# A second feed-forward whose split of g is issued one step later, with the last check and the last stores moved

## The chip, the cores and the metric

The kernel runs on one core of one Trainium2 chip. The metric is the device time of one execution in microseconds. TensorE multiplies matrices into PSUM; ScalarE and VectorE do element-wise work and copy results out of PSUM; GpSimd issues gathers; SyncE (SP) issues most of the other transfers. Each engine works through its own list of instructions, in the order of the program, and waits for the others by semaphores.

## The reference

Three parts follow one another: a gated linear attention, a mixture of eight experts with the best two for each token, and a second feed-forward. The change lies in the last.

```python
def _moe2_ref(x, w_in, w_out):       # x: 3072 x 384, w_in: 384 x 2048, w_out: 2048 x 384
    h = x @ w_in
    g = h - np.tanh(h)
    return (g @ w_out).astype(np.float32)

attn_out = _attn_ref(**attn_kwargs)  # 4 x 8 heads, 768 tokens, 48 wide
x = attn_out.transpose(0, 2, 1, 3).reshape(3072, 384)
x = _moe_ref(x=x, **moe_kwargs)      # 8 experts, 1024 wide, best 2 of each token
return _moe2_ref(x=x, **moe2_kwargs)
```

## The kernel before

The function `fast` holds all three parts. Numbers are kept as pairs of 16-bit halves, a high one and a low one that holds the rest, so that a product takes three 16-bit matmuls: high by high, high by low, low by high.

The second feed-forward cuts the 3072 tokens into six blocks of 512 (`blk`) and the 2048 hidden columns into sixteen groups of 128 (`f`). That gives M = 96 steps, numbered n = 16 blk + f. In step n:

- `ff_first` makes the **first products**: nine matmuls of 512 columns on TensorE (line 185) into a PSUM bank `ph`. Four banks take turns. ScalarE then makes `z` from `ph` (line 637, with a sum over the columns into `hsum`), and `s` from `z` (638). VectorE makes `s` (639) and `g` (641). z(n), s(n), g(n) are those of step n.
- `ff_split` splits `g`: ScalarE writes the **high half** of the tile `hs` (line 647), then VectorE the **low half** (648). Four tiles `hs` take turns.
- `ff_second` makes the **second products** of step n - 3 (FF_LAG = 3): twelve matmuls of 384 columns (line 200), three for each of four groups of 128 tokens, into the banks `py0` to `py3`. The third of each three reads the low half. After f = 15 the block is done: the four banks are copied to tiles `o`, two by ScalarE (line 665) and two by VectorE (663), and each is stored by a transfer that SP issues (666). The next block's second products for f = 0 need the same four banks.
- Then come extras of the step: `combine`, `put_m` and `sum_m` prepare the tokens of the next block and sum them, `weight_sum` (line 149) sums weights, and in the last block one piece of `checks` a step tests the value ranges.

Order on an engine is program order, which the loop at the end of `fast` writes out by hand. first(n) and second(n) are the two kinds of product of step n; the second feed-forward starts behind the last step of the experts, and steps 0 to 3 have first products ahead of second(0).

When the last step's sums are there, `last_check` makes one column `ok` in six small VectorE operations; a tiny matmul counts it, and VectorE writes `flag` (line 816). All engines load the flag (line 1064) and branch on it (1065): where a check fails, a general version (`general`) runs behind the branch. In every execution here it is jumped over.

Of the kernel before, what the change touches and what calls it, by code (L numbers as in the profile page):

```python
# [20 lines left out]
B, H, S, D = 4, 8, 768, 48  # L21
N, DM, NE, FF, F2 = 3072, 384, 8, 1024, 2048
# [44 lines left out]
def rows(ap, offset, pattern):  # L67
    return bass.AP(tensor=ap.tensor, offset=ap.offset + offset, ap=pattern)
# [3 lines left out]
def fast(ctx, tc, flag, f_cols, kq_cols, v_rows, gates, blank, w12, w_in, w_out, out):  # L72
    nc = tc.nc
# [12 lines left out]
    ones = consts.tile([128, 128], BF, name="ones")  # L86
# [61 lines left out]
    def weight_sum(e, f, i):  # L148
        nc.scalar.activation(junk[:, :DM], RING[e, f][:, 0, 3 * i:3 * i + 3, :].rearrange("p a b -> p (a b)"),  # L149
                             AF.Square, accum_out=wsum[:, 8 * e + f, i:i + 1])  # L150
# [17 lines left out]
    def new_xt(key):  # L168
        XT[key] = xtp.tile([128, 6, 512], F16, name="xt")
# [9 lines left out]
    def first_products(ph, n, lhs, key):  # L179
        x = XT[key]  # L180
        o = 0
        for a in range(3):
            wh, wl = lhs(a)
            for l, r in ((wh, a), (wh, 3 + a), (wl, a)):
                nc.tensor.matmul(ph[:, :n], l, x[:, r, :n], start=(o == 0), stop=(o == 8))  # L185
                o += 1

    def second_products(key, f, last, rhs, parts):
        hs = HS.pop((key, f))
        wh, wl = (w.rearrange("p a b -> p (a b)") for w in rhs)  # L190
        for i, (c0, m) in enumerate(parts):
            if f == 0:
                PY[key, i] = ps.tile([128, DM], F32, name=f"py{i}", tag=("b0", "b1", "b2", "b5")[i])
            p = PY[key, i]
            if m == 64:
                ops = [(hs[:, c0:c0 + 2 * m], w) for w in (wh, wl)]
            else:
                ops = [(hs[:, s + c0:s + c0 + m], w) for s, w in ((0, wh), (0, wl), (512, wh))]
            for o, (l, r) in enumerate(ops):
                nc.tensor.matmul(p[:max(m, 128)], l, r, start=(f == 0 and o == 0),  # L200
                                 stop=(f == last and o == len(ops) - 1))
# [401 lines left out]
    YG = {}  # L603

    def gather_y(j):
        g1, g2 = (late.tile([128, DM], F32, name=f"g{r}", bufs=6) for r in range(2))
        for r, g in ((0, g1), (1, g2)):
            nc.gpsimd.indirect_dma_start(out=g, out_offset=None, in_=y_rows if j > 3 else y_rows[:Y_EARLY],  # L608
                                         in_offset=bass.IndirectOffsetOnAxis(ap=yslot[:, r, j:j + 1], axis=0))
        YG[j] = (g1, g2)  # L610

    def combine(j):
        g1, g2 = YG.pop(j)
        nc.scalar.activation(g1, g1, AF.Copy, scale=wt[:, 0, j:j + 1])  # L614
        nc.vector.scalar_tensor_tensor(g1, g2, wt[:, 1, j:j + 1], g1, op0=OP.mult, op1=OP.add)
        YG[j] = g1

    def put_m(j):
        g1 = YG.pop(j)
        m = late.tile([128, 2 * DM], F16, name="m16")  # L620
        nc.scalar.activation(m[:, :DM], g1, AF.Copy)
        nc.vector.tensor_tensor(m[:, DM:], g1, m[:, :DM], op=OP.subtract)
        c = 128 * (j % 4)
        nc.sync.dma_start_transpose(XT["m", j // 4][:, :, c:c + 128], m)
        YG[j] = g1

    def sum_m(j):
        nc.scalar.activation(junk[:, :DM], YG.pop(j), AF.Square, accum_out=msum[:, j:j + 1])  # L628

    def ff_first(blk, f):  # L630
        ph = ps.tile([128, 512], F32, name="ph", tag=next(tags["ph"]))
        first_products(ph, 512, lambda a: (winS[:, 0, a, f * 128:(f + 1) * 128],
                                           winS[:, 1, a, f * 128:(f + 1) * 128]), ("m", blk))
        z = ff.tile([128, 512], F32, name="z")
        s = ff.tile([128, 512], F32, name="s")
        i = blk * 16 + f
        nc.scalar.activation(z, ph, AF.Square, scale=SZ ** 0.5 / SH, accum_out=hsum[:, i:i + 1])  # L637
        nc.scalar.activation(s, z, AF.Square, scale=1.0 / SZ, bias=bias_a)  # L638
        nc.vector.scalar_tensor_tensor(s, s, ZD, z, op0=OP.add, op1=OP.mult)  # L639
        g = ff.tile([128, 512], F32, name="g")  # L640
        nc.vector.scalar_tensor_tensor(g, s, 0.5, ph, op0=OP.mult, op1=OP.mult)  # L641
        YG["g", blk, f] = g

    def ff_split(blk, f):
        g = YG.pop(("g", blk, f))
        hs = tiles.tile([128, 1024], F16, name="hs", bufs=4)
        nc.scalar.activation(hs[:, :512], g, AF.Copy)  # L647
        nc.vector.tensor_tensor(hs[:, 512:], g, hs[:, :512], op=OP.subtract)  # L648
        HS[("m", blk), f] = hs

    def ff_second(blk, f):
        w = RING[NE, f // 2]
        c = 3 * (f % 2)
        second_products(("m", blk), f, 15, (w[:, 0, c:c + 3, :], w[:, 1, c:c + 3, :]),
                        [(128 * i, 128) for i in range(4)])
        if f < 15:
            return
        for i in range(4):
            c, b = divmod(4 * blk + i, B)
            o = ff.tile([128, DM], F32, name="o", bufs=4)  # L660
            p = PY.pop((("m", blk), i))
            if i % 2:
                nc.vector.tensor_scalar(o, p, 2.0 * C2 / (SH * SZ * SW), None, op0=OP.mult)
            else:
                nc.scalar.activation(o, p, AF.Copy, scale=2.0 * C2 / (SH * SZ * SW))  # L665
            nc.sync.dma_start(rows(out, (b * S + c * 128) * DM, [[DM, 128], [1, DM]]), o)

    todo = [(1, i) for i in range(32)] + [(0, 8 * a + c) for c in range(8) for a in range(3)]
    loads_ahead = list(todo)
# [1 line left out]
    for n in range(3, len(moe_steps) + LAG):  # L671
# [3 lines left out]
        e, blk, f = moe_steps[n]  # L675
# [52 lines left out]
    def holds(i, src, bound, op):  # L728
        t = held[:, :src.free_size()]
        if len(src.shape) > 2:  # L730
            t = t.rearrange("p (a b) -> p a b", b=src.shape[2])
        nc.vector.tensor_scalar(t, src, bound, None, op0=op)
        nc.vector.tensor_reduce(okay[:, i:i + 1], held[:, :src.free_size()], axis=AX.X, op=OP.min)
# [5 lines left out]
    def check(i, src, bound, op):  # L739
        holds(i, src, bound, op)  # L740
        both(okay[:, i:i + 1])
# [48 lines left out]
    def last_check():  # L790
        check(2, hsum[:, 90:], HMIN2 * SZ, OP.is_ge)
        holds(3, hsum[:, 90:], HMAX2 * SZ, OP.is_le)
        ok = consts.tile([128, 1], BF, name="ok")
        nc.vector.tensor_tensor(ok, okay[:, 0:1], okay[:, 3:4], op=OP.mult)
        return ok
# [3 lines left out]
    FF_LAG = 3  # L799
    steps = [(blk, f) for blk in range(6) for f in range(16)]  # L800
    M = len(steps)
    halves = [(e, f, i) for e in (NE - 1, NE) for f in range(8) for i in range(2)]
    checking = checks()
    for n in range(M + FF_LAG):
        if n < M:
            blk, f = steps[n]
            ahead = 4 * blk + 4
            if blk < 5 and f == 0:
                for i in range(4):
                    gather_y(ahead + i)  # L810
                new_xt(("m", blk + 1))
            ff_first(blk, f)
        if n == M + FF_LAG - 1:
            p = ps.tile([1, 1], F32, name="pt", tag="b7")
            nc.tensor.matmul(p, ok, ones[:, 0:1], start=True, stop=True)
            nc.vector.tensor_scalar(flag, p, 128.0, None, op0=OP.is_lt)
        if n >= FF_LAG:
            ff_second(*steps[n - FF_LAG])
        if n >= M:
            continue  # L820
        ff_split(blk, f)
        if blk < 5:
            if f in (1, 3, 5, 7):
                combine(ahead + f // 2)
            if f in (2, 4, 6, 8):
                put_m(ahead + f // 2 - 1)
            if f in (9, 10, 11, 12):
                sum_m(ahead + f - 9)
        else:
            next(checking, None)  # L830
        if halves and (blk == 5 or f == 0 or f > 12):
            weight_sum(*halves.pop(0))
        if n < 2:
            sum_m(2 * n)
            sum_m(2 * n + 1)
        if n == M - 1:
            ok = last_check()


@with_exitstack  # L840
# [218 lines left out]
def fused_kernel(tc, args, packed, out):  # L1059
    nc = tc.nc  # L1060
    with tc.tile_pool(name="flags", bufs=1) as flags:
        flag = flags.tile([1, 1], I32, name="flag")
        fast(tc, flag, *packed, *args[-2:], out)
        again = nc.values_load(flag, min_val=0, max_val=1)
        with tc.If(again > 0):
            general(tc, *args, out)
# [54 lines left out]
```

## Time and profile before

| | us |
|---|---|
| median of 3 runs | 971.24 |
| lowest and highest run | 967.05, 971.27 |
| the profiled execution, its own time | 962.48 |
| its span in the trace | 960.7 |
| TensorE busy | 938.4 (98%) |
| VectorE busy | 616.0 (64%) |
| ScalarE busy | 611.2 (64%) |
| GpSimd busy | 160.5 (17%) |

The trace is of one execution, whose own time is less than that of all three runs that were timed without a profile. The second feed-forward runs from about 568 us to the end of the span. In the rows PE is TensorE, PEld its weight loads, ACT ScalarE, DVE VectorE, POOL GpSimd and SP SyncE. A name with a q (SPq) is the engine's queue of instructions that are not counted as busy: issues of transfers, semaphores, branches. "Idle before" is how long an engine stood before an instruction, and the arrow names what ended the wait. The granted clock of TensorE is 1.00 at its full speed.

### The profile page before, as it was taken

To read this page: it belongs to the slowest core of one execution; us is meant where nothing else is said; L and a number is where in the kernel's file an instruction comes from. 1 tells how busy PE (TensorE), PEld (TensorE's weight loads), DVE (VectorE), ACT (ScalarE), POOL (GpSimd) and SP (SyncE) were. 2 spreads that over 40 slices of the span, in tenths; PEclk is the share of its full clock that TensorE was granted. 3 is DMA by queue.
4 is the path that set the end of the run, shared out by engine and by line. 5 is a ranking of instruction groups with operands and counts; after the bars stand their busy time and mean duration, and the time that the engine had idled before them with its cause. 6 is when DMAs were issued, how large, how long until landed. Compare 5 with 4: busy or idle time off the path is not lost.

```text
span 960.7 us, 16309 instructions
## 1 busy us (share of the span) xinstructions
PE 938.4 (98%) x5970; PEld 576.5 (60%) x5970; DVE 616.0 (64%) x1274; ACT 611.2 (64%) x1593; POOL 160.5 (17%) x194
## 2 busy tenths in 40 slices
PE   8999998999999999999999999979999999999996
PEld 8999986555656565656556554535555555555553
DVE  8999995466464646566666556556566565665764
ACT  7777763575757575776767566666665666666663
POOL 2387786000000000000000223200301201000000
PEclk9999999999999999999999999989999999999999
DMA  7877855756565456564645354212222121110001
GB/s 274 286 248 252 263 166 170 200 176 167 153 177 149 161 143 187 151 157 134 186 122 136 99 149 103 64 34 44 74 42 47 44 58 42 42 26 1 33 1 37
DMA packets 111801, 120.03 MB, mean 125 GB/s; under 512 B 66400, under 2 KB 89568, under 8 KB 111584
## 3 DMA queue, kind: packets, MB, share of 16 engines
q1 hardware_dynamic: 105568, 100.03, 36.4%
q0 software_dynamic: 6144, 18.88, 6.3%
q8 instruction: 48, 0.79, 0.3%
q14 instruction: 41, 0.34, 0.1%
HBM read 76.41 MB, written 29.88 MB: 111 GB/s over the span
## 4 chain that ended last, share of the span: by engine, by line
PE 60%; ACT 21%; DVE 14%; issue 1%; DMA 1%; POOL 0%; SPq 0%; DVEq 0%; ACTq 0%
PE py L200 24%; PE ph L185 23%; ACT s L638 6%; DVE s L639 6%; DVE g L641 6%; ACT hs L647 5%; ACT z L637 5%; PE pY L366 4%; PE pA L339 2%; PE pt L410 2%; PE pY L364 2%; PE pK L383 2%; ACT junk L628 1%; ACT junk L149 1%; ACT g L614 1%
## 5 line engine op out<-in xcount | busy, mean ns | idle before, releaser
L200 PE MATMUL py<-wsplit,hs 128*128 128x384 f16 x2432 | 433.8, 327 | 7.2 <-ACT o L665 5.6
L200 PEld LDWEIGHTS <-hs 128*128 128x128 f16 x2432 | 237.0, 98 | 181.3 <-issue 9.2
L185 PE MATMUL ph<-xt,wsplit 128*128 128x512 f16 (+3 forms) x1152 | 223.5, 339 | 0.4 <-DMA xt<-xs 0.4
L185 PE MATMUL ph<-xt,winS 128*128 128x512 f16 x864 | 201.7, 379 | 0.0
L185 PEld LDWEIGHTS <-wsplit 128*128 128x128 f16 x1152 | 112.5, 98 | 86.7 <-DMA xt<-xs 0.8
L218 DVE SCALAR_TENSOR_TENSOR hs<-ph,hs 128x256 f16<-128x256 f32 (+2 forms) x192 | 79.6, 443 | 119.1 <-ACT hs L210 118.9
L608 POOL DMA_INDIRECT g<-y_rows,yslot x48 | 52.7, 1097 | 585.1 <-ACT wsplit L144 376.0
L210 ACT ACTIVATE hs<-ph 128x512 f16<-128x512 f32 (+3 forms) x128 | 65.8, 514 | 132.6 <-PE ph L185 132.6
L647 ACT ACTIVATE hs<-g 128x512 f16<-128x512 f32 x96 | 60.4, 629 | 138.5 <-DVE g L641 138.5
L185 PEld LDWEIGHTS <-winS 128*128 128x128 f16 x864 | 84.4, 98 | 92.0
L639 DVE SCALAR_TENSOR_TENSOR s<-s,z 128x512 f32<-128x512 f32 x96 | 66.5, 692 | 80.9 <-ACT s L638 80.9
L648 DVE TENSOR_TENSOR hs<-g,hs 128x512 f16<-128x512 f32 x96 | 66.4, 692 | 63.3 <-ACT hs L647 61.9
L145 DVE SCALAR_TENSOR_TENSOR wsplit<-raw,wsplit 128x768 f16<-128x768 f32 x72 | 70.3, 976 | 16.3 <-ACT wsplit L144 15.0
L149 ACT ACTIVATE junk<-wsplit 128x384 f16<-128x384 f16 x144 | 74.4, 516 | 2.3
L638 ACT ACTIVATE s<-z,bias_a 128x512 f32<-128x512 f32 x96 | 69.3, 722 | 3.1
L641 DVE SCALAR_TENSOR_TENSOR g<-s,ph 128x512 f32<-128x512 f32 x96 | 65.9, 687 | 3.3
L144 ACT ACTIVATE wsplit<-raw 128x768 f16<-128x768 f32 x72 | 59.9, 832 | 0.3 <-DMA raw<-wo_f 0.3
L479 POOL DMA_INDIRECT xs<-xkeep,yslot x48 | 55.7, 1161 | 15.8 <-issue 8.7
L637 ACT ACTIVATE z<-ph 128x512 f32<-128x512 f32 x96 | 55.4, 577 | 2.0 <-PE ph L185 1.9
L366 PE MATMUL pY<-v,am 128*128 128x48 f32 x384 | 53.3, 267 | 0.0
L366 PEld LDWEIGHTS pY<-v,am 128*128 128x128 f32 x384 | 49.6, 192 | 0.1
L325 POOL TENSOR_TENSOR kqT<-eneg,kq 128x512 f32<-128x512 f32 x23 | 32.0, 1392 | 16.0 <-ACT eneg L321 15.7
(135 smaller groups left out, 904.9 us busy)
## 6 DMA issues: line engine op xcount, KB each, us to landing
raw<-in_w SPq DMA_DIRECT2D x64, 384.0 KB, 3.8
kq<-in_kq_cols SPq DMA_DIRECT2D x24, 512.0 KB, 5.8
y_rows<-yo SPq DMA_DIRECT2D x47, 192.0 KB, 1.9
f<-in_f_cols SPq DMA_DIRECT2D x24, 256.0 KB, 4.3
w<-in_moe_w_out SPq DMA_DIRECT2D x32, 192.0 KB, 3.4
w<-in_moe_w_in SPq DMA_DIRECT2D x24, 256.0 KB, 3.4
v<-in_v_rows SPq DMA_DIRECT2D x24, 192.0 KB, 3.2
out<-o SPq DMA_DIRECT2D x24, 192.0 KB, 2.0
```

What stands on the lines that cost most here:

```text
L145: nc.vector.scalar_tensor_tensor(t[:, 1], raw, SW, t[:, 0], op0=OP.mult, op1=OP.subtract)
L149: nc.scalar.activation(junk[:, :DM], RING[e, f][:, 0, 3 * i:3 * i + 3, :].rearrange("p a b -> p (a b)"), AF.Square, accum_out=wsum[:, 8 * ...
L185: nc.tensor.matmul(ph[:, :n], l, x[:, r, :n], start=(o == 0), stop=(o == 8))
L200: nc.tensor.matmul(p[:max(m, 128)], l, r, start=(f == 0 and o == 0), stop=(f == last and o == len(ops) - 1))
L218: nc.vector.scalar_tensor_tensor(hs[:, at:at + hi - lo], ph[:, lo:hi], 0.0, hs[:, lo:hi], op0=OP.max, op1=OP.subtract)
L366: nc.tensor.matmul(pY[:, at + 48 * s:at + 48 * s + 48], am[:, s, a, :], vt[:, 2 * a + s, :], start=not c, stop=bool(s) or not c)
L637: nc.scalar.activation(z, ph, AF.Square, scale=SZ ** 0.5 / SH, accum_out=hsum[:, i:i + 1])
L638: nc.scalar.activation(s, z, AF.Square, scale=1.0 / SZ, bias=bias_a)
L639: nc.vector.scalar_tensor_tensor(s, s, ZD, z, op0=OP.add, op1=OP.mult)
L641: nc.vector.scalar_tensor_tensor(g, s, 0.5, ph, op0=OP.mult, op1=OP.mult)
L647: nc.scalar.activation(hs[:, :512], g, AF.Copy)
L648: nc.vector.tensor_tensor(hs[:, 512:], g, hs[:, :512], op=OP.subtract)
```

## The change

Three edits in the second feed-forward. The split of step n - 1 is issued in step n, behind the first products and the element-wise work of step n and ahead of the second products of step n - 3. `last_check` is issued inside the last `ff_first`, behind the last z and s of ScalarE and ahead of the last s of VectorE; the matmul on its result and the write of the flag come one step earlier, ahead of second(94). And the stores of the last block that belong to ScalarE's copies are issued by ScalarE.

```diff
@@ ff_first
         nc.scalar.activation(s, z, AF.Square, scale=1.0 / SZ, bias=bias_a)
+        if i == 95:
+            YG["ok"] = last_check()
         nc.vector.scalar_tensor_tensor(s, s, ZD, z, op0=OP.add, op1=OP.mult)
@@ ff_second
-            nc.sync.dma_start(rows(out, (b * S + c * 128) * DM, [[DM, 128], [1, DM]]), o)
+            (nc.sync if i % 2 or blk < 5 else nc.scalar).dma_start(
+                rows(out, (b * S + c * 128) * DM, [[DM, 128], [1, DM]]), o)
@@ the loop over n
             ff_first(blk, f)
-        if n == M + FF_LAG - 1:
+        if 0 < n <= M:
+            ff_split(*steps[n - 1])
+        if n == M + FF_LAG - 2:
             p = ps.tile([1, 1], F32, name="pt", tag="b7")
-            nc.tensor.matmul(p, ok, ones[:, 0:1], start=True, stop=True)
+            nc.tensor.matmul(p, YG["ok"], ones[:, 0:1], start=True, stop=True)
             nc.vector.tensor_scalar(flag, p, 128.0, None, op0=OP.is_lt)
         if n >= FF_LAG:
             ff_second(*steps[n - FF_LAG])
         if n >= M:
             continue
-        ff_split(blk, f)
...
-        if n == M - 1:
-            ok = last_check()
```

The lines behind the edits move by two or three: what is 647, 648, 663, 665 and 816 before is 649, 650, 665, 667 and 821 after.

**ScalarE at the end of block 0.** The rows are those of the steps n = 17 and 18; `py0` and `py2` hold the results of block 0, `g0` and `m16` are tiles of the extras. Before:

```order
L637 ACTIVATE z_7417,hsum_92<-ph_7407 128x512
L638 ACTIVATE s_7418<-z_7417,bias_a_74 128x512
L647 ACTIVATE hs_7436<-g_7422 128x512
L614 ACTIVATE g0_7357<-g0_7357,wt_91 128x384
L637 ACTIVATE z_7451,hsum_92<-ph_7441 128x512
L638 ACTIVATE s_7452<-z_7451,bias_a_74 128x512
L665 ACTIVATE o_7470<-py0_6929 128x384
L665 ACTIVATE o_7476<-py2_6937 128x384
L647 ACTIVATE hs_7482<-g_7456 128x512
L621 ACTIVATE m16_7485<-g0_7357 128x384
```

After:

```order
L637 ACTIVATE z_7414,hsum_92<-ph_7404 128x512
L638 ACTIVATE s_7415<-z_7414,bias_a_74 128x512
L649 ACTIVATE hs_7421<-g_7386 128x512
L614 ACTIVATE g0_7354<-g0_7354,wt_91 128x384
L637 ACTIVATE z_7448,hsum_92<-ph_7438 128x512
L638 ACTIVATE s_7449<-z_7448,bias_a_74 128x512
L649 ACTIVATE hs_7455<-g_7419 128x512
L667 ACTIVATE o_7470<-py0_6929 128x384
L667 ACTIVATE o_7476<-py2_6937 128x384
L621 ACTIVATE m16_7482<-g0_7354 128x384
```

In step 17 the high half is now that of the step before (it reads `g_7386`, not the `g_7419` of its own step), and in step 18 it stands ahead of the two copies `o`, where it stood behind them.

**VectorE at the same place.** `s_7452` (before) and `s_7449` (after) are those of n = 18. Before:

```order
L639 SCALAR_TENSOR_TENSOR s_7452<-s_7452,z_7451 128x512
L641 SCALAR_TENSOR_TENSOR g_7456<-s_7452,ph_7441 128x512
L663 TENSOR_SCALAR o_7473<-py1_6933 128x384
L663 TENSOR_SCALAR o_7479<-py3_6941 128x384
L648 TENSOR_TENSOR hs_7482<-g_7456,hs_7482 128x512
L622 TENSOR_TENSOR m16_7485<-g0_7357,m16_7485 128x384
```

After:

```order
L641 SCALAR_TENSOR_TENSOR s_7449<-s_7449,z_7448 128x512
L643 SCALAR_TENSOR_TENSOR g_7453<-s_7449,ph_7438 128x512
L650 TENSOR_TENSOR hs_7455<-g_7419,hs_7455 128x512
L665 TENSOR_SCALAR o_7473<-py1_6933 128x384
L665 TENSOR_SCALAR o_7479<-py3_6941 128x384
L622 TENSOR_TENSOR m16_7482<-g0_7354,m16_7482 128x384
```

The low half has moved ahead of the two copies `o` and belongs to the step before.

**VectorE at the end.** These are the rows from the last check inside the steps to the flag; `hsum` 128x6 marks the moved check, and the `s` behind it is that of n = 95. Before:

```order
L737 TENSOR_TENSOR okay_6819<-okay_6819 128x1
L639 SCALAR_TENSOR_TENSOR s_10244<-s_10244,z_10243 128x512
L641 SCALAR_TENSOR_TENSOR g_10248<-s_10244,ph_10233 128x512
L648 TENSOR_TENSOR hs_10262<-g_10248,hs_10262 128x512
L732 TENSOR_SCALAR held_6820<-hsum_92 128x6
L733 TENSOR_REDUCE okay_6819<-held_6820 128x1
L737 TENSOR_TENSOR okay_6819<-okay_6819 128x1
L732 TENSOR_SCALAR held_6820<-hsum_92 128x6
L733 TENSOR_REDUCE okay_6819<-held_6820 128x1
L794 TENSOR_TENSOR ok_10270<-okay_6819 128x1
L816 TENSOR_SCALAR flag_58<-pt_10296 1x1
```

After:

```order
L740 TENSOR_TENSOR okay_6819<-okay_6819 128x1
L735 TENSOR_SCALAR held_6820<-hsum_92 128x6
L736 TENSOR_REDUCE okay_6819<-held_6820 128x1
L740 TENSOR_TENSOR okay_6819<-okay_6819 128x1
L735 TENSOR_SCALAR held_6820<-hsum_92 128x6
L736 TENSOR_REDUCE okay_6819<-held_6820 128x1
L797 TENSOR_TENSOR ok_10249<-okay_6819 128x1
L641 SCALAR_TENSOR_TENSOR s_10241<-s_10241,z_10240 128x512
L643 SCALAR_TENSOR_TENSOR g_10252<-s_10241,ph_10230 128x512
L650 TENSOR_TENSOR hs_10254<-g_10207,hs_10254 128x512
L650 TENSOR_TENSOR hs_10269<-g_10252,hs_10269 128x512
L821 TENSOR_SCALAR flag_58<-pt_10284 1x1
```

The six operations of the check now stand ahead of the last s and g, and the low halves of n = 94 and n = 95 follow these in a row.

## Rows read from the trace of the kernel before

**Rows 1.** The page, part 1: busy us (share of span) x instructions.
```profile
PE 938.4 (98%) x5970; PEld 576.5 (60%) x5970; DVE 616.0 (64%) x1274; ACT 611.2 (64%) x1593; POOL 160.5 (17%) x194
```

**Rows 2.** Waits, whole span: engine, line, released by; us in total, times, longest.
```profile
ACT hs L647 <- DVE g L641: 138.5, 96, 1.8
...
PE py L200 <- ACT o L665: 5.6, 1, 5.6
...
PE py L200 <- DVE o L663: 0.9, 3, 0.4
```

**Rows 3.** Timeline around 640 us: start, duration, engine, line, operation, count, [idle before].
```profile
637.95 2.11 PE L185 MATMUL ph<-xt,winS 128*128 128x512 f16 x9
...
643.82 0.58 ACT L637 ACTIVATE z<-ph 128x512 f32<-128x512 f32 x1
...
644.52 0.72 ACT L638 ACTIVATE s<-z,bias_a 128x512 f32<-128x512 f32 x1
...
645.15 0.85 ACT L665 ACTIVATE o<-py 128x384 f32<-128x384 f32 x2
...
645.67 1.12 PE L200 MATMUL py<-wsplit,hs 128*128 128x384 f16 x3 [5.62 <-ACT o L665]
...
649.59 2.10 PE L185 MATMUL ph<-xt,winS 128*128 128x512 f16 x9
```

**Rows 4.** Windows: length, busy us of PE, PEld, DVE, ACT, POOL; granted clock; DMA.
```profile
10.00:15.00 5.00, 3.59 (x53) 3.29 (x51) 4.92 (x8) 3.68 (x8) 1.28 (x1) 1.00 0.96 354
...
645.70:649.50 3.80, 3.38 (x12) 1.52 (x12) 3.33 (x7) 2.64 (x6) 0.00 (x0) 0.55 0.54 193
```

**Rows 5.** Timeline: second products nine steps apart.
```profile
651.53 2.12 PE L200 MATMUL py<-wsplit,hs 128*128 128x384 f16 x12
...
686.56 2.11 PE L200 MATMUL py<-wsplit,hs 128*128 128x384 f16 x12
```

**Rows 6.** Groups by line, 650 to 940 us: busy us, mean ns, idle before.
```profile
L641 DVE SCALAR_TENSOR_TENSOR g<-s,ph 128x512 f32<-128x512 f32 x75 | 51.5, 687 | 2.6
...
L648 DVE TENSOR_TENSOR hs<-g,hs 128x512 f16<-128x512 f32 x74 | 51.2, 692 | 48.7 <-ACT hs L647 48.0 <-PE ph L185 0.7
...
L647 ACT ACTIVATE hs<-g 128x512 f16<-128x512 f32 x74 | 46.6, 629 | 106.5 <-DVE g L641 106.5
```

**Rows 7.** Timeline at the start of the second feed-forward.
```profile
571.48 0.72 ACT L638 ACTIVATE s<-z,bias_a 128x512 f32<-128x512 f32 x1
...
574.21 0.51 ACT L149 ACTIVATE junk<-wsplit 128x384 f16<-128x384 f16 x1
...
576.01 0.58 ACT L637 ACTIVATE z<-ph 128x512 f32<-128x512 f32 x1
...
576.38 2.12 PE L200 MATMUL py<-wsplit,hs 128*128 128x384 f16 x12
...
587.05 2.11 PE L185 MATMUL ph<-xt,winS 128*128 128x512 f16 x9
```

**Rows 8.** Timeline of the end, VectorE.
```profile
949.20 0.16 DVE L732 TENSOR_SCALAR held<-hsum 128x6 f32<-128x6 f32 x1
...
950.06 0.16 DVE L794 TENSOR_TENSOR ok<-okay 128x1 bf16<-128x1 f32 x1
...
952.72 0.56 DVE L663 TENSOR_SCALAR o<-py 128x384 f32<-128x384 f32 x1 [0.42 <-PE py L200]
```

**Rows 9.** Tile `o`, 940 to 961 us: issues on SP (ns min/median/max), landing.
```profile
L666 SPq DMA_DIRECT2D out<-o x4: 332/362/1784, 951.8 to 954.6; - x4
...
DMA to landing us min/median/max: 2.3/3.7/3.8
```

**Rows 10.** Instructions of line 1065: ns min/median/max, first and last start.
```profile
L1065 SPq COMPARE_BRANCH  x1: 58/58/58, 955.1 to 955.1; - x1
...
L1065 SPq EVENT_SEMAPHORE  x8: 17/17/17, 957.9 to 958.5; - x8
...
L1065 DVEq EVENT_SEMAPHORE  x1: 21/21/21, 956.7 to 956.7; - x1
```

## The prediction

> **What bounds the kernel now.** I read the busy shares first. TensorE is busy for 938.4 us of a span of 960.7 us [rows 1], so only what makes it stop, or run slowly, is to be had. Next I read who makes it wait. One wait stands out: 5.62 us, once, in the second products (line 200), for ScalarE's copy `o` (line 665). VectorE's copies `o` cost 0.9 us in three waits. ScalarE itself waits 138.5 us in 96 pieces, once in every step, at line 647 for VectorE's `g` [rows 2]. That is a round trip inside each step: ScalarE makes z and s, VectorE s and g, ScalarE returns for the high half of `hs`, VectorE makes the low half.
>
> The timeline at the large wait shows what the round trip does [rows 3]. Count the steps of the feed-forward as n = 16 blk + f. TensorE makes the first products of n = 19 from 637.95 to about 640.05. It then needs the bank that block 0 left, and that is copied by a ScalarE instruction queued behind z and s of n = 18. z of n = 18 starts at 643.82, though its products were made one step earlier, before 636.1: ScalarE is 7.7 us late. The copy starts at 645.15, and TensorE resumes at 645.67. Until 649.59 its 12 products run at a granted clock of 0.55 [rows 4], that is at or near the lower of TensorE's two levels (1.2 and 2.4 GHz). So 640.05 to 649.59, 9.54 us, were spent on work that takes 1.95 us: 7.6 us lost.
>
> The undisturbed step is read between the second products that start at 651.53 and at 686.56, nine steps apart [rows 5]: 35.03/9 = 3.892 us, half of it for each kind of product. ScalarE's round trip takes about as long: z to s 0.70 us, s to the next instruction 0.63 [rows 3], three VectorE operations of 0.69 and the high half 0.63 [rows 6], partly beside the next z, plus some 0.6 us of a combine or a sum. So once late it stays late. Where it fell behind is the start: TensorE makes four first products in a row, and ScalarE's step 0 carries three extra sums [rows 7].
>
> **The change, part by part.**
>
> *The split one step later.* No operation is added; in step n ScalarE runs z(n), s(n), hs(n-1), then the step's extra. g(n-1) is ready long before, so the 138.5 us of waiting go. ScalarE's step is then 0.70 + 0.63 [rows 3] + 0.63 [rows 6] + about 0.6 for the extra (three sums in 1.80 us [rows 7]), 2.6 us against 3.892, and a lag of 7.7 us cannot last: it shrinks by 1.3 us in each of the 14 steps to the first block end.
>
> What is late next? Let T be the end of first(n), and ScalarE on time. z at T, s at T+0.70, hs(n-1) at T+1.33 to 1.96. VectorE: s at T+1.45, g at T+2.17, the low half of hs(n-1) from T+2.89 to 3.58. So the low half of hs(n), made in step n+1, is ready at T+3.89+3.58 = T+7.5. TensorE wants it with the third product of second(n), at T + 3 x 3.892 + 0.33 = T+12.0. Hidden, with 4.5 us to spare.
>
> At a block's end the four copies `o` now stand behind the split, as the orders above show. ScalarE's first runs from T+1.96 to 2.5, VectorE's first from T+3.61 to 4.17 (0.56 us each [rows 8]). TensorE wants the first bank at T+3.89, the second 0.49 us later, at T+4.38. Both fit, the second by 0.2 us only; if the margin goes I price it at 0.3 us per block end. Gain at the first block end: **7.6 us**. The later ends wait 0.9 - 0.42 = 0.5 us today; I keep 0.2 of it: **0.3 us**.
>
> *The start.* second(0) begins at 576.38. Today the five groups from there to 587.05 take 10.67 us where 2.5 steps are 9.73: 0.94 lost [rows 7]. After: ScalarE's three sums take 576.01 - 574.21 = 1.80 us and follow s(0) at 571.48 + 0.63 = 572.11; z(1) starts at 573.91, s(1) at 574.61, hs(0) at 575.24. VectorE does s(1) at 575.36, g(1) at 576.08, the low half of hs(0) from 576.80 to 577.49. The third product, due at 576.71, waits 0.8 us, and behind it on TensorE stands first(4). By the same sums lo(1) is ready at 581.1 for a third product at 581.4, and z(5) is on time. So 0.8 for 0.94: **0**. The bounds are 0.9 won (no wait) and 1.0 lost (the low half as late again). The clock stays if this wait is like those of 10 to 15 us, where TensorE was busy 3.59 of 5 us and was granted 1.00 [rows 4].
>
> *The last check.* Six small VectorE operations, 949.20 to 950.22, 1.02 us [rows 8], move ahead of the last s. They wait for the sum of the last z; behind them stand s(95), g(95) and the low half of hs(94), for which second(94) waits. With T the end of first(95), step 94's own low half ends at T-0.3, its six check operations at T+0.7, the moved six at T+1.75, s and g by T+3.19, the low half at T+3.9; second(94) wants it at T+3.89+0.33 = T+4.22. **0**, covered by second(92) and second(93); without the cover up to 1.0 us. The flag's tiny matmul moves one step up at the same price.
>
> *The last stores.* Four issues on SP, three of some 0.36 us and one of 1.78 us; the last starts at 954.6, and data lands 2.3 to 3.8 us after an issue [rows 9]. SP's compare-and-branch follows at 955.1, its first semaphore after the jump at 957.9; VectorE gets there at 956.7 [rows 10]. With two of the four on ScalarE's queue, SP issues its last behind VectorE's last copy (952.72 + 0.56 = 953.28), is done at 953.7, and passes its jump 2.8 us later, at 956.6. VectorE's 956.7 is then last: 957.9 - 956.7 = 1.2 us. A store issued at 953.3 lands at the latest at 957.1, which leaves 0.8. I take **1.1 us**. No row shows an issue on ScalarE. Nearest are the issues on SP, 0.33 to 1.78 us; if both on ScalarE take 1.78, its jump ends near 959.4, so 1.5 us lost. I take 0.36, the same transfer in the other three, and keep the ends. The page "DMA: Bandwidth & Descriptors" of the Trainium skill (section "Issuing engines are not separate DMA queues") says that all issuing engines share the same 16 DMA engines, and that a second one saves only the time of issuing, usually little; by it this part would give two issues of 0.36, 0.7 us, not 1.1.
>
> **Sum**: 7.6 + 0.3 + 0 + 0 + 1.1 = 9.0 us. The profiled execution's own time is 962.48 us (960.7 of span), so it would take 953.5. The median shown is 8.8 us above that execution, and no row says why; I take the same 9.0 us from it: 971.24 - 9.0 = **962.2 us**. With all low bounds the gain is 7.6 - 0.7 (0.3 lost at four ends, beyond the 0.5 there today) - 1.0 - 1.0 - 1.5 = 3.4, with all high ones 7.6 + 0.5 + 0.9 + 0 + 1.2 = 10.2: 961.0 to 967.8.
>
> **The rivals.**
>
> *The stall stays* (the change does not do what it says): ScalarE stays late into the first block end because something else holds it there, say the gathers that the combines read. For it: the lag of today lasted 14 steps. Against: of the 74 steps from 650 us on, the row of the high half shows 106.5 us of waiting, all of it for `g` [rows 6], and that is what the change takes away. Only the 1.1 us of the stores are left: 970.1.
>
> *The start costs the clock.* The wait of second(0) grows from 0.8 us towards the 5.6 that were seen to bring the lower clock. The page "TensorE: Matmul & The Clock Gate" (part 1) has an idle TensorE fall to 1.2 GHz; the stall's products agree (0.55 granted). Price: second(0)'s 12 products as slow as those, 3.8 for 1.95 us, and 1 us more of waiting: 2.9 us less, 965.1. For it: only 0.3 us of slack behind lo(1). Against: the 1.4 us at full clock.
>
> *Slower.* The copies `o` stand behind one ScalarE and one VectorE operation more. If ScalarE were late as today at each of the five block ends, every end would stall: 7.7 + 2.5 - 3.9 = 6.3 us, and 1.9 for the clock, five times 8.2 = 41 against today's 8.1. So +33 less the 1.1: 1003. It decides where ScalarE's step exceeds 3.892 us, and by the sum above it is 2.6.
>
> **How the numbers follow.** The forecast has 0.77, the stall that stays 0.11, the start's clock 0.07, the slower case 0.03; 0.02 stays for what I have not seen. About half a per cent, 4.9 us, is what a measurement of this kernel can tell from no change. Faster takes the forecast (all but its low end, 0.75) and the start's case, 0.82; the same takes the stall that stays and what is left of the forecast, 0.14; slower 0.04. The likeliest one's own range is 961.0 to 967.8. Runs of the kernel before spread from 967.05 to 971.27, so the lower end is 967.05 - 9.0 = 958, and the upper end stays at 968, short of the stall that stays.
>
> **What would show it.** Right: no TensorE wait for `o` above 0.3 us and the granted clock at 1.00 around 640 us; ScalarE no longer waiting for `g` at the split; z starting as its first products end by n = 5; second(0) waiting some 0.8 us for the low half; the last SP issue 0.6 us after the last copy starts (today 1.9), and some 6.9 us from that copy to the end of the span (today 8.0). Wrong: a wait for `o` of microseconds at any block end; a granted clock under 1 behind second(0); an issue on ScalarE above 1 us; a wait of second(94) for VectorE.

## The result

The changed kernel takes 957.41 us (median of nine runs, 955.33 to 964.77); the kernel before, beside it on the same chip, took 967.05 us (nine runs, 964.54 to 971.27). The ratio is 0.9899, 95% interval 0.9875 to 0.9923: faster by 1.0%. The forecast was 962.2 us in a range of 958.0 to 968.0, so the time lies 0.6 us under the range. The difference of the medians is 9.6 us, and 9.0 was forecast: the gain came as forecast, from a base that was set too high. The forecast started from 971.24 us, the median of three runs; they are the first three of the nine, and two of them turned out to be the two longest.

The profiled execution takes 957.17 us with a span of 955.4. TensorE's busy time, and the engines on the chain that ended last:

```profile
PE 940.5 (98%) x5970; PEld 581.3 (61%) x5970; DVE 607.8 (64%) x1274; ACT 610.8 (64%) x1593; POOL 156.7 (16%) x194
...
PE 94%; DVE 2%; issue 1%; ACT 1%; DMA 1%; POOL 1%; SPq 0%; DVEq 0%; POOLq 0%; ACTq 0%
```

The chain is now TensorE almost alone. The waits of 560 to 956 us (engine, line, released by; us in total, times, longest) answer to [rows 2]:

```profile
ACT z L637 <- PE ph L185: 131.3, 90, 5.7
...
ACT hs L649 <- DVE g L643: 1.1, 1, 1.1
PE py L200 <- DVE hs L650: 0.8, 2, 0.6
...
PE py L200 <- issue: 0.2, 1, 0.2
```

TensorE no longer waits for any copy `o`: the 5.6 and the 0.9 us are gone. ScalarE's 138.5 us of waiting for `g` have become 1.1, and it stands 131.3 us ahead of `z` instead, for TensorE. Waiting for the engine that bounds the kernel costs nothing; waiting in the middle of a round trip did. The timeline at the end of block 0 answers to [rows 3]:

```profile
640.23 2.11 PE L200 MATMUL py<-wsplit,hs 128*128 128x384 f16 x12
...
640.43 0.60 ACT L637 ACTIVATE z<-ph 128x512 f32<-128x512 f32 x1 [1.43 <-PE ph L185]
...
641.78 0.61 ACT L649 ACTIVATE hs<-g 128x512 f16<-128x512 f32 x1
...
642.18 2.11 PE L185 MATMUL ph<-xt,winS 128*128 128x512 f16 x9
...
642.30 0.85 ACT L667 ACTIVATE o<-py 128x384 f32<-128x384 f32 x2
...
643.84 1.01 DVE L665 TENSOR_SCALAR o<-py 128x384 f32<-128x384 f32 x2
...
644.12 2.11 PE L200 MATMUL py<-wsplit,hs 128*128 128x384 f16 x12
```

z of n = 18 starts as its products end, where it was 7.7 us late. The split and the two copies follow in the order forecast, and VectorE's first copy is done at 644.40; TensorE, which starts the group at 644.12, needs that bank 0.49 us later, at 644.61. The margin is the forecast 0.2 us. The window of [rows 4], in the changed kernel:

```profile
645.70:649.50 3.80, 3.80 (x23) 1.97 (x21) 2.51 (x4) 2.34 (x6) 0.00 (x0) 1.00 0.61 166
```

TensorE is busy throughout at a granted clock of 1.00, where it was 0.55. The start, to be read beside [rows 7]:

```profile
580.15 0.49 PE L200 MATMUL py<-wsplit,hs 128*128 128x384 f16 x2
...
581.20 1.80 PE L200 MATMUL py<-wsplit,hs 128*128 128x384 f16 x10 [0.56 <-DVE hs L650]
...
590.62 2.10 PE L185 MATMUL ph<-xt,winS 128*128 128x512 f16 x9
```

second(0) does its first two products and stands 0.56 us for the low half. Its five groups take 590.62 - 580.15 = 10.47 us against 10.67. The last stores and the jump to the end, beside [rows 8 to 10], in three views. VectorE's last copy in the timeline:

```profile
948.23 0.56 DVE L665 TENSOR_SCALAR o<-py 128x384 f32<-128x384 f32 x1 [0.42 <-PE py L200]
```

The issues of the tile `o`, 940 to 956 us (ns min/median/max, first and last start):

```profile
L668 ACTq DMA_DIRECT2D out<-o x2: 338/360/381, 947.3 to 948.3; - x2
L668 SPq DMA_DIRECT2D out<-o x2: 332/336/341, 947.8 to 948.8; - x2
```

And the instructions of the jump, line 1067:

```profile
L1067 SPq EVENT_SEMAPHORE  x8: 17/17/17, 953.2 to 953.7; - x8
...
L1067 DVEq COMPARE_BRANCH  x1: 72/72/72, 949.0 to 949.0; - x1
L1067 SPq COMPARE_BRANCH  x1: 58/58/58, 949.2 to 949.2; - x1
...
L1067 DVEq EVENT_SEMAPHORE  x1: 21/21/21, 953.3 to 953.3; - x1
```

No issue takes above 0.38 us, and SP reaches its branch at 949.2, 1.0 us after the last copy starts (2.4 before). But its first semaphore behind the jump comes 4.0 us later, where it was 2.8.

Cut at the start of the second feed-forward (its first products) and at the last copy `o`, the two profiled executions compare so: start to last copy 384.11 to 375.85 us (-8.26), last copy to the end of the span 7.98 to 7.17 (-0.81), together -9.07. What lies ahead of the second feed-forward, which the change does not touch, took 3.77 us longer (its first products start at 572.38 against 568.61); the part on the base, at the end of the experiments, comes to that.

### The profile page after: what moved, and what is told of

Read it like the earlier page. It is cut to its first block, busy times and chain, and to the rows that moved or that the text cites. A ratio compares the mean times of both kernels' runs of the same rounds, so it can differ in the third digit from the quotient of the medians.

```text
span 955.4 us, 16329 instructions
## 1 busy us (share of the span) xinstructions
PE 940.5 (98%) x5970; PEld 581.3 (61%) x5970; DVE 607.8 (64%) x1274; ACT 610.8 (64%) x1593; POOL 156.7 (16%) x194
## 4 chain that ended last, share of the span: by engine, by line
PE 94%; DVE 2%; issue 1%; ACT 1%; DMA 1%; POOL 1%; SPq 0%; DVEq 0%; POOLq 0%; ACTq 0%
PE py L200 40%; PE ph L185 39%; PE pY L366 4%; PE pA L339 2%; PE pY L364 2%; PE pK L383 2%; PE pt L410 2%; PE pkr L352 1%; PE pK L492 1%; POOL xs L479 1%; PE pE L398 1%; DMA xt<-xs 0%; DMA xs<-xkeep,yslot 0%; DVE am L341 0%; DVE fc L312 0%
## 5 line engine op out<-in xcount | busy, mean ns | idle before, releaser
L608 POOL DMA_INDIRECT g<-y_rows,yslot x48 | 47.8, 996 | 579.4 <-ACT wsplit L144 375.7
L637 ACT ACTIVATE z<-ph 128x512 f32<-128x512 f32 x96 | 57.2, 596 | 131.3 <-PE ph L185 131.3
```

## The experiments

Ratios are to the kernel before, run on the same chip in the same session. "Feed-forward" is the time from its first products to the last copy `o`, "tail" from there to the end of the span.

**The split alone.**

```diff
             ff_first(blk, f)
+        if 0 < n <= M:
+            ff_split(*steps[n - 1])
...
-        ff_split(blk, f)
```

> Only the split is issued one step later; the check and the stores are as before. My theory (ScalarE, late by 7.7 us, pays 7.6 us once at the end of block 0, and the later split frees it): 7.6 to 8.3 us below the kernel before, ratio 0.991 to 0.993, no TensorE wait for a copy o above 0.3 us, granted clock 1.00 around 640 us, and from the last copy o to the end of the span some 8.0 us as before. Rival, the gain lies at the end (stores and check): ratio 0.999 to 1.001 and the wait of 5.6 us is still there.

959.52 us (six runs), ratio 0.990 (0.9852 to 0.9947). Feed-forward 375.95 us, tail 8.0; no wait for `o`. The whole gain inside the feed-forward is the split's; the tail is that of before.

**The stores alone**, on two queues in the last block, as in the change.

> Only the last block's stores on two queues. Theory: 0.8 to 1.1 us less than before, ratio 0.999, which this measurement can hardly tell from 1; in the trace the last copy o to the end of the span takes 7.0 to 7.2 us in place of 8.0, and the wait of 5.6 us at the end of block 0 stays. Rival, the issue of 1.78 us on SP is a matter of one execution and not of the queue: then the stretch is 7.0 to 7.2 us only where no such issue falls, and kernels with all four stores on SP show it too.

966.49 us (twelve), ratio 0.998 (0.9953 to 1.0008). Feed-forward 384.58, tail 8.0. The issues are short (none above 0.68 us), and yet the tail did not shrink in this profile to the 7.0 to 7.2 us expected: SP branches at 958.1 and has its semaphore at 961.1, VectorE at 957.5 and 960.9, ScalarE at 957.9 and 961.2. All three jump within 0.6 us of each other and take 3.0 to 3.4 us.

**The last check alone**, inside the last step, its matmul one step earlier.

> Only the last check ahead of the last s, and the flag one step earlier. Theory: hidden behind second(92) to second(94), ratio 1.000 within 0.001, no wait of TensorE for VectorE in the last four second products, the wait of 5.6 us at the end of block 0 stays. Rival, the check stood on the path that ends last: 1 us less.

966.11 us (twelve), ratio 0.9974 (0.9943 to 1.0006). Feed-forward 386.17, tail 8.2. Nothing that this measurement can tell; the profile shows no wait of TensorE at the moved check.

**Where the lag comes from: a lighter start of the kernel before.** The four sums of tokens and one sum of weights of the steps 0 and 1 are made ahead of the second feed-forward; the split stays where it was.

```diff
+    weight_sum(*halves.pop(0))
...
-        if n < 2:
-            sum_m(2 * n)
-            sum_m(2 * n + 1)
```

> The split as before, but the five sums that ScalarE runs in steps 0 and 1 of the second feed-forward are issued earlier, behind the last steps of the experts. Theory (the start makes ScalarE late, and its round trip, as long as TensorE's step, keeps it so): z(1) starts some 1.8 us and z(2) some 3 us earlier, so ScalarE is 4.7 us late at the end of block 0 in place of 7.7, and the wait for the copy o is 2.6 to 3.3 us in place of 5.6; 3 to 5 us less than before, ratio 0.995 to 0.997. Rival, the lag is made in the steps of block 0 (combines and sums longer than TensorE's step): the wait stays near 5.6 us, ratio 0.999 to 1.001.

964.73 us (twelve), ratio 0.9959 (0.993 to 0.9988), feed-forward 382.36. From z(0) to z(18) ScalarE takes 70.14 us against 73.06, so it comes to the block end 2.9 us earlier, counted from z(0). The waits of 560 to 956 us:

```profile
PE py L200 <- ACT o L665: 3.9, 1, 3.9
...
PE py L200 <- DVE o L663: 1.0, 3, 0.4
```

The wait alone shows nothing, for it is as short in two kernels whose start was left alone: 3.9 us with the stores alone and 3.8 with the check alone, where TensorE had already stood 1.7 and 1.8 us for no releaser that the trace names, some 20 us into the feed-forward. What holds still is ScalarE's own time. In all five profiles with the split and the start of before (before, the two single edits above, and the two kernels of before with fills below) it takes 73.06 to 73.08 us from z(0) to z(18), and TensorE starts second(16), the products behind the wait, 77.05 to 77.07 us after first(0), while the wait for `o` is anything from 0.7 to 5.6: what TensorE loses earlier it does not wait for later. Here the two stretches are 70.14 and 74.14 us. So work of the first two steps is paid for sixteen steps later: the lag is carried, as the prediction read it.

**The same load on both.** Ten copies of 128x512, 6.56 us together in the kernel before, are added to ScalarE in step 8 (their result is not used), once in the kernel before, once in the changed one.

```diff
+        if n == 8:
+            for _ in range(10):
+                nc.scalar.activation(junk, winS[:, 0, 0, 0:512], AF.Copy)
```

> The kernel before with ten more copies of 128x512 on ScalarE behind step 8 of the second feed-forward, about 5 us of extra work there that nothing needs. Theory: ScalarE cannot make up time while its step holds the round trip, so TensorE, which is already at the limit of its lead, waits for nearly all of it once: 4 to 6 us more than before, ratio 1.004 to 1.006, and the wait for the copy o at the end of block 0 stays. Rival, ScalarE has 36% of idle time and takes the work in: ratio 0.999 to 1.001.

> The changed kernel with the same ten copies behind step 8. Theory: the low half has 4.5 us to spare and ScalarE makes up 1.3 us in each step, so TensorE waits 0 to 1 us, the lag is gone by step 13, and the time is that of the changed kernel plus 0 to 1 us: ratio to the kernel before 0.990 to 0.992. Rival, the later split only moves the time at which ScalarE is late and makes up nothing: 4 to 6 us more than the changed kernel, ratio 0.994 to 0.997.

Before: 974.55 us (ten), ratio 1.0068 (1.0042 to 1.0094), feed-forward 390.09 (+6.0):

```profile
PE py L200 <- ACT hs L647: 4.7, 2, 4.3
PE py L200 <- ACT o L665: 3.5, 1, 3.5
```

The ratio is a little above the 1.004 to 1.006 expected. Changed kernel: 955.23 us (four), ratio 0.985 (0.9797 to 0.9903), feed-forward 375.38, not more than the 375.85 without the load:

```profile
PE py L200 <- DVE hs L650: 0.9, 2, 0.6
...
610.31 0.58 ACT L637 ACTIVATE z<-ph 128x512 f32<-128x512 f32 x1
...
612.66 0.57 ACT L637 ACTIVATE z<-ph 128x512 f32<-128x512 f32 x1
```

z(9) to z(12) start at 610.31, 612.66, 615.02 and 617.62, 2.35 to 2.6 us apart, until ScalarE has caught up. This is the experiment that tells the theory from its rivals: the same extra work costs the kernel before 6 us, and the changed one a wait of 0.3 us that its time does not show, because there a late ScalarE runs at its own step of some 2.4 us (2.6 forecast) until it is on time.

**The lighter start on the changed kernel.**

> The changed kernel with the five sums of steps 0 and 1 issued earlier, behind the last steps of the experts. Theory: the low half of step 0 is then ready before second(0) wants it, and the wait of 0.6 us there goes: 0.5 to 1.0 us less than the changed kernel, ratio to the kernel before 0.988 to 0.990; in the trace no wait of TensorE for VectorE's low half in the first 30 us of the second feed-forward. Rival: the sums now hold up the last products of the experts, and the time is that of the changed kernel or more.

956.71 us (six), ratio 0.9891 (0.9846 to 0.9937); feed-forward 374.15, 1.7 us less than the changed kernel, with no wait of TensorE for another engine in it. Of the 1.7 us, 0.7 lie in the five groups at the start (9.73 us against 10.47) and 1.0 in two steps around 594 us, where only the changed kernel's execution has a hole on ScalarE (last section). The wait at the start is real and small; the total can't tell it from none.

**One step further: the split two steps late** (a third buffer for `g`).

```diff
-        if 0 < n <= M:
-            ff_split(*steps[n - 1])
+        if 1 < n <= M + 1:
+            ff_split(*steps[n - 2])
```

> The changed kernel with the split two steps late in place of one, and three buffers for g. Theory: the low half is ready 11.4 us after its first products and wanted after 12.0, so the steady steps still lose nothing, 0.6 us to spare; but second(0) waits some 3.7 us in place of 0.6: 3 to 5 us more than the changed kernel, ratio to the kernel before 0.993 to 0.996. Rival, 0.6 us is less than the extras of a step on VectorE (a combine is 0.6 us), and steps with extras wait too: some 0.3 us in each of 40 steps, ratio above 1.

964.98 us (ten), ratio 0.997 (0.9931 to 1.0008), feed-forward 381.72, 5.9 more than one step late:

```profile
PE py L200 <- ACT hs L649: 3.2, 1, 3.2
PE py L200 <- DVE hs L650: 2.3, 2, 1.2
```

The first wait and 1.0 us of the second lie at the start. The other 1.2 us lie at the end, in the second products of step 93 (timeline, TensorE):

```profile
947.04 1.80 PE L200 MATMUL py<-wsplit,hs 128*128 128x384 f16 x10 [1.22 <-DVE hs L650]
```

VectorE makes their low half in step 95, behind the moved check, and TensorE wants it sooner than in the steps before, since no first products stand between second(92) and second(93); how the 1.2 us part between the two is not separated. No step between waits. One step late is enough to break the round trip; a second one only brings waits at both ends.

**The base: what lifts a run above the best ones.** Nine of the ten profiles so far (all but before's) show a low granted clock at 140 to 165 us, in the last steps of the attention, ahead of anything the change touches. Windows of before, then of the changed kernel (length, busy us of PE, PEld, DVE, ACT, POOL; granted clock; DMA):

```profile
150.00:155.00 5.00, 3.78 (x33) 3.42 (x32) 1.29 (x6) 1.99 (x6) 4.12 (x9) 1.00 0.45 169
155.00:160.00 5.00, 4.61 (x34) 3.16 (x34) 2.98 (x16) 2.36 (x7) 3.21 (x7) 1.00 0.42 158
```

```profile
150.00:155.00 5.00, 3.78 (x26) 3.42 (x25) 1.15 (x6) 1.99 (x6) 4.13 (x9) 0.85 0.44 164
155.00:160.00 5.00, 5.00 (x24) 4.15 (x24) 0.55 (x3) 0.87 (x2) 4.04 (x8) 0.50 0.43 160
160.00:165.00 5.00, 5.00 (x36) 3.37 (x35) 3.32 (x19) 2.15 (x8) 1.05 (x2) 0.97 0.10 39
```

TensorE is busy for the same 3.78 us in both, between waits of 0.54 to 0.66 us for ScalarE and VectorE; in one execution it keeps its full clock behind them, in the other it falls to 0.50, the lower level (1.2 GHz). With 0.97 in the five us that follow, the changed kernel's windows miss 0.15, 0.50 and 0.03 of 5 us each, 3.4 us by estimate, which is most of the 3.77 us that it starts its second feed-forward later. In the nine profiles that start is at 571.3 to 576.4 us, in before's at 568.61. Over 91 later runs of the kernel before, time goes with the mean granted clock (correlation -0.88): nine runs at 0.981 or less have a median of 976.0 us, 22 at 0.984 to 0.987 one of 970.2, 18 at 0.988 to 0.990 one of 969.1, 42 at 0.991 and above one of 966.8.

To test whether the short waits bring the clock down, they were filled with small matmuls of 128x128 on a tile of ones, whose results are not read. First in groups of eight, ahead of each product of the last steps:

```diff
+            if j >= 21:
+                warm(8)
             scores(j + 1)
...
+            if j >= 21:
+                warm(8)
             if j:
                 logits(j - 1)
...
+            if j >= 20:
+                warm(8)
             x_transposed(j)
```

> The kernel before with 64 to 88 small matmuls of 128x128 on a tile of ones, added in the last attention steps (about 130 to 165 us), where TensorE stands in gaps of 0.54 to 0.66 us behind ScalarE and VectorE; their results are not read. Theory: the runs of before spread because in most executions the granted clock falls to about half at 150 to 163 us, which costs 3 to 5 us; the median of three on which the forecast stood (971.24) holds that loss and the profiled execution (962.48) does not. Filled gaps keep the clock at 1.00 there: median about 964 us against 968, ratio 0.995, spread down from 13 us to some 6, first products of the second feed-forward at 568 to 570 us. Rival: the spread is from elsewhere and the added matmuls only take TensorE's time: ratio 1.000 to 1.003, spread as before.

> The changed kernel with the same added matmuls. Theory: clock 1.00 from 130 to 165 us, first products of the second feed-forward at 568 to 570 us (572.4 without), median about 953 to 954 us, ratio to before 0.986. Rival: clock or start unchanged, median 957, ratio 0.990, or worse by the 3 us that the added matmuls take where they are not hidden.

> The changed kernel with the added matmuls and with the lighter first steps (the four sums of tokens and the sum of weights of steps 0 and 1 made ahead or later). Theory: the two gains are in different stretches and add: no wait of second(0) (0.8 us won) and the clock at 1.00 around 150 us, median about 952.5 to 953.5 us, ratio 0.985. Rival: as the changed kernel, 957 us, 0.990.

Before with fills: 973.93 us (twelve), ratio 1.0032 (1.0008 to 1.0056). Changed kernel with fills: 967.04 (twelve), 0.9982 (0.996 to 1.0003); with the lighter start too: 962.86 (six), 0.993 (0.9904 to 0.9957). All three missed. In each one group of fills, right behind another on the same bank, stood itself, in the changed kernel:

```profile
156.70 1.01 PE L492 MATMUL pK<-ones 128*128 128x128 bf16 x8 [3.70 <-remote]
```

2.3, 3.7 and 2.3 us in the three profiles, and the clock fell behind that (0.58 to 0.83 in the window of 5 us that holds its end). What held it the trace does not name. So these runs do not tell the theories apart; they say that the fills were badly placed. The repair has six groups of six, only where the trace of before shows a wait, and no two in a row:

```diff
+            if j in (21, 22):
+                warm(6)
             scores(j + 1)
...
+            if last:
+                warm(6)
             if j:
                 logits(j - 1)
...
+            if j in (20, 21, 22):
+                warm(6)
             x_transposed(j)
```

> The kernel before with six fills of six small matmuls each (128x128 on a tile of ones, results not read), only where its own trace shows TensorE standing 0.2 to 0.66 us behind ScalarE and VectorE at 138 to 152 us, and no two in a row on one bank, where the first attempt stood 2.3 to 3.7 us. Theory (the short waits bring the lower clock at 150 to 163 us, and that is what lifts the median of before above its best runs): granted clock 1.00 from 130 to 170 us, first products of the second feed-forward at 569 to 571 us, ratio 0.995 to 0.997, and fewer runs above 970. Rival (the waits are not what brings the clock down, or the spread is from elsewhere): ratio 1.000 to 1.003, runs as widely spread as those of before.

> The changed kernel with the same six fills. Theory: clock 1.00 from 130 to 170 us, first products of the second feed-forward at 569 to 571 us (572.4 without), median some 3 us below the changed kernel, ratio to before 0.985 to 0.987. Rival: ratio 0.990 to 0.993.

Before: 969.16 us, ratio 0.9996 (0.9977 to 1.0015). Changed kernel: 959.82 (six), 0.9903 (0.9873 to 0.9932). The medians did not fall, and the first products of the second feed-forward start at 575.5 and 574.5 us, not at 569 to 571 as expected. But the spread fell: eleven of the twelve runs of before lie between 968.41 and 969.41 us, where seventeen without fills, in the same session, lie between 964.93 and 975.49; five of the six of the changed kernel lie between 959.41 and 960.54. The windows of before with fills:

```profile
150.00:155.00 5.00, 4.45 (x44) 4.09 (x44) 1.02 (x5) 1.99 (x6) 4.12 (x9) 1.00 0.41 155
155.00:160.00 5.00, 2.67 (x21) 1.83 (x19) 0.21 (x3) 0.00 (x0) 4.01 (x8) 1.00 0.42 157
160.00:165.00 5.00, 2.12 (x9) 1.37 (x10) 2.78 (x16) 1.83 (x5) 0.00 (x0) 0.52 0.11 39
```

And its timeline, ScalarE and TensorE:

```profile
161.07 0.49 ACT L369 ACTIVATE x<-pY 128x384 f32<-128x384 f32 x1 [6.64 <-remote]
...
162.69 0.20 PE L444 MATMUL pt<-sel,before 128*128 128x24 bf16 x1 [5.02 <-DVE sel L436]
```

The clock stays at 1.00 over the filled waits. Then ScalarE stands 6.64 us ahead of a copy (line 369) whose products ended near 156.2, VectorE's `sel` comes late behind it, TensorE stands 5.02 us, and the clock falls to 0.52 there instead. The loss that some runs had and some not seems to be one that nearly all now have, of about the median's size; only one execution of each kernel was traced, so this is read from the spread. The two kernels with fills differ by 969.16 - 959.82 = 9.34 us with little spread: the cleanest reading of what the change is worth.

## Why the gain was right and the time was not

**The base.** This is the step that failed: "The median shown is 8.8 us above that execution, and no row says why; I take the same 9.0 us from it", and after it the range's lower end, "the lower end is 967.05 - 9.0 = 958". Three runs did not show how far runs reach, and that two of them were the longest of nine was bad luck. The base measured 967.05 us where 971.24 was taken: 4.2 us of the 4.8 by which the forecast is off, and the gain, 9.6 for 9.0, is the rest. The kernel before gave medians of 967.05 to 969.71 in five sessions, and single runs from 962.75 to 977.76. The profiled execution less 9.0, 953.5 us, stood in the working and outside the range, though it was the only run whose inside could be read; with it as the lower end the range would have held 957.41. As the base it would have failed the other way: its 962.48 us is below every one of the 101 timed runs of that kernel, and 953.5 is 3.9 below the measured time. What the runs showed in the base's place: time goes with the granted clock, part of it is lost at 140 to 165 us in most executions, and the profile of before is one without that loss.

**The stall**, 7.6 us and 0.3 at later block ends: 7.9 forecast, 8.26 measured in the profiles and 8.16 with the split alone. Over more profiles without an added load or a lighter start, the feed-forward takes 383.90 to 386.17 us in five with the split of before and 375.85 to 378.93 in four with it one step late. The reasons held one by one: in the kernel before z(8) to z(18) start 3.93 us apart, no shorter than TensorE's step of 3.89; the waits for `g` went, the lag shrinks by itself (shown by the ten added copies), and the copies fit with the forecast margin. One sign came late: z starts as its products end from n = 8 on, not from n = 5, since ScalarE's hole ahead of z(5) made it 5.35 us late once more; three steps made that up. The rival that the stall stays fell with the first rows, the slower one with them.

**The start**, 0: TensorE waits 0.56 us where 0.8 was forecast, and the five groups take 0.2 us less than before. No clock was lost there, against the second rival.

**The last check**, 0: the tiny matmul runs at 944.02 and the products of the steps 94 and 95 follow at 944.12 without a wait; alone it changed nothing that can be told.

**The last stores**, 1.1 forecast, 0.81 measured. ScalarE's issues cost the 0.36 us assumed. Off was "passes its jump 2.8 us later": SP took 4.0, and VectorE 4.3 instead of 3.2. Their jumps and ScalarE's now fall within 0.4 us of each other; that this makes them longer is not shown, for with the stores alone they fell within 0.6 us and took 3.0 to 3.4. Single profiles scatter here. Over all fifteen, seven with four stores on SP have a mean tail of 8.21 us and eight with two queues one of 7.24, 1.0 us less. But seven of these eight also have the split and the check moved, and each edit alone left the tail at 8.0 to 8.2, so the shorter tail belongs to the edits together, and how much of it is the stores' stays open. The Trainium skill's page "DMA: Bandwidth & Descriptors" (section "Issuing engines are not separate DMA queues") has a second issuer save only the time of issuing; the 0.7 us that the prediction works out from it is an estimate, and the means differ by 1.0. In all seven profiles with four stores on SP the slowest of them took 1.10 to 2.36 us to issue, and in none of the other eight did one take above 0.68.

**What stays open**: what holds ScalarE ahead of line 369, and whether the short waits alone bring the clock down. The fills speak for it (clock and spread), and against it stands the profile of before, which had the same waits and kept its clock; a version without the later stall was not found, so it is not settled.

## What to carry to other kernels

A wait that repeats in every step on an engine that is not the bound is harmless only until something makes that engine late: read whether its step, with the round trip, is shorter than the bound's step, for only then does a lag shrink; issuing the returning half one step later takes the round trip out, and a second step cost 5.9 us of that here. A forecast of a time needs a base as much as a gain: where the profiled execution and the timed runs differ by more than the gain is uncertain, say which the profile stands for, and let the range hold both; the median of three runs can lie anywhere in the spread.

## What was unexpected on this chip

- The jumps at the end are not of a fixed price: 2.8 us for SP and 3.2 for VectorE where they came 1.6 us apart, 4.0 and 4.3 where three engines jumped within 0.4 us, and 3.0 to 3.4 where they did so within 0.6. What sets it is open.
- Of four stores that SP issues in a row the slowest takes 1.10 to 2.36 us to issue where the first takes 0.34, in every profile with four of them; in two of the seven a second one took 1.01 and 1.53.
- ScalarE has holes of 4 to 7 us for which the trace names no work that was late. In the changed kernel there is one ahead of z(5), whose products were done by 588.9 (timeline, ScalarE):

```profile
594.18 0.60 ACT L637 ACTIVATE z<-ph 128x512 f32<-128x512 f32 x1 [5.75 <-PE ph L185]
```

TensorE's two steps there took together 1.0 us more than the 3.89 us of the others, and no more, since a step late is now caught up; ahead of line 369, where TensorE came to wait on the chain behind it, it stood 5.0. They come and go between executions and kernels that differ only elsewhere; I did not find what holds ScalarE there.
